# Batch 0 of a state-attention and Mish kernel: slot 0 in halves, low words rounded by GpSimd, steps in another order

## The chip, the cores and the metric

The kernel runs on one core of a Trainium2 chip. Its metric is device time in microseconds (us) of one execution. Engines are named as in the profile: PE is TensorE, PEld its weight loads, DVE VectorE, ACT ScalarE, POOL GpSimd, SP SyncE, which here issues the transfers.

## The reference, cut to what matters

```python
def _attn_ref(x, state):                     # x [8, 8, 512, 64], state [8, 8, 32, 64]
    scores = scale * x @ state^T             # softmax over the 32 states: a
    xread = a @ state                        # 512 rows of each batch
    scores2 = scale * state @ x^T            # softmax over the 512 tokens: a2
    sread = a2 @ x                           # 32 rows of each batch
    return concatenate([xread, sread], axis=2)

def _moe_ref(x, w_in, w_out):                # x [4352, 512]: the above, heads side by side
    h = x @ w_in                             # w_in [512, 2048], given as 64-bit floats
    g = h * tanh(softplus(h))                # Mish
    return g @ w_out                         # w_out [2048, 512], given as 64-bit floats
```

Eight batches of 512 + 32 rows go through the attention and then through the two products.

## The kernel before, in words

**Products.** The hidden width of 2048 is cut into 8 slots of 256 columns. For a batch and a slot the first product is not `xread @ w_in`: the kernel multiplies the state with the slot's columns of `w_in` (a slice, `sw`, tiles `swp`, `swh`, `swl`) and then with the softmax weights (tiles `ah`, `al`). Every fp32 operand of the big products is split into a high and a low part of type fp32r, and a product is three matmuls: high x high, high x low, low x high. The first product of a slot (`gemm1`, tiles `ph`) is two halves of 128 hidden columns with 6 matmuls of 512 columns each, in two PSUM banks (`ps_h`, two buffers). Mish (`take_g`, ScalarE) turns each half into its half of `g`; VectorE splits `g` into `gh` and `gl` (`high_g`, `low_g`). The second product (`gemm2`, tiles `acc`) adds the slot to four accumulators, one for each 128 tokens: 4 x 6 matmuls with the slot's `w_out`, itself split (`wo`).

**Weights.** `w_in` and `w_out` come as 64-bit floats, seen as pairs of 32-bit words. Once, during batch 0, every slot's share of each (1 MB, 128 x 1024 pairs) is turned into fp32 in three steps: ScalarE scales the high word (`scale_high`), an engine rounds the low word (`round_low`, an instruction over every second word), and VectorE joins the two (`join_words`, which reads both). `w_out` is then split by VectorE (`high_w_out`, `low_w_out`); `w_in` goes into the slices. SP issues the loads in one order: x of batch 0, `wir` 0, `wor` 0, `wir` 1, `wir` 2, `wor` 1, `wir` 3, `wor` 2, `wir` 4, `wor` 3, `wir` 5, x of batch 1, `wor` 4, 6, 5, `wir` 6, 7, `wor` 7. `wir` 4 to 7 reuse the buffers of `wir` 0, 1, 4, 5 and wait until these have been joined; `wor` 6 and 5 lie where `wir` 2 and 3 were.

**Batch 0 is an order written out by hand.** `InOrder` chains the instructions of PE, DVE and ACT in the order in which the Python code issues them. The code walks a list of step names; a step that is a generator goes on to its next `yield` each time its name comes. In a name, letters stand for the work and the number for the slot:

- `x`, `st`, `sc`, `tr`, `ex`, `no`, `pr`: attention of batch 0 (transposing x and the state, scores, exponentials, norms, weights `ah` and `al`); in capitals that of batch 1; `mm`, `ee`, `et`, `sr`, `rt`: its other softmax and `sread`
- `hi`, `ho`: high words of `w_in` or `w_out` (ScalarE); `ci`, `co`: low words by ScalarE; `di`, `do`: by VectorE; `ji`, `jo`: joining (`jo` comes twice, the second time for the high part); `lo`: low part of `w_out`
- `sw`: a slice (PE, then ScalarE's `swh`, then VectorE's `swl`); `p`: first product; `m`: Mish, then `gh`; `lg`: `gl`; `g`: one token tile of the second product; `next`: the first slice of batch 1
- `fillN`: N matmuls into an accumulator that is written anew later

In the order before, all low words but `di2`, `do1` and `do2` are rounded by ScalarE, and `fill6` stands between `p0` and `p1`.

**From batch 1 on** a loop over batches (`key`) and slots (`j`) issues the work. Besides the products, a slot may have a *visit*: slices (`sw_slice`), scores (`sc`), transposes (`et`) or `sread` matmuls (`sr`) of this or the next batch, which PE runs between the two halves of a slot's second product. In batch 1 the visits are those of slots 1 (slice 2), 2 (`et`), 3 (slice 4 and `sr`), 4 (`sc`), 5 (slice 6), 6 and 7.

The numbers in front of the lines are those of the profile. Nearly all instructions are recorded at L66, where `InOrder` issues them, so groups are told apart by their tiles.

Of the kernel before, what the change touches and what calls it, by code (L numbers as in the profile page):

```python
# [73 lines left out]
def state_attention_mish_kernel(ctx, tc, x, state, w_in, w_out, out):  # L74

    nc = tc.nc
    pe, dve, act = (InOrder(tc, e) for e in (nc.tensor, nc.vector, nc.scalar))
    nc.scalar.preload_act_table_set("exp_and_others")
# [71 lines left out]

    def round_low(raw, by_vector=False):
        lw = raw[..., 0]
        if by_vector:
            dve.tensor_scalar(lw, lw, 0.876 * 2.0 ** -29, 0.49, ALU.mult, ALU.add)
        else:
            last["words"] = act.activation(lw, lw, AF.Copy, scale=0.876 * 2.0 ** -29, bias=0.49)

    def join_words(raw, to):
        lw, hw = raw[..., 0], raw[..., 1]
        last["join"] = dve.scalar_tensor_tensor(  # L160
            to.bitcast(U32), hw, 3, lw, ALU.logical_shift_left, ALU.bitwise_or)
# [25 lines left out]

    def join_w_out(j, raw):
        w = pool.tile([P, 2, DM], F32, tag="wt", name=f"w_{j}", bufs=1)
        join_words(raw, w)  # L190
        return w

    def high_w_out(j, w):
        wo[j] = const.tile([P, 2, 2, DM], F32R, tag=f"wo{j}", name=f"wo_{j}")
        last["woh"] = dve.tensor_copy(wo[j][:, :, 1], w)
# [310 lines left out]
    def split_g(key, g):  # L506
        gh, gl = high_g(key, g)
        low_g(g, gh, gl)
        return gh, gl

    def high_g(key, g):
        gh = pool.tile([P, W], F32R, tag="gh", name=f"gh_{key}")
        gl = pool.tile([P, W], F32R, tag="gl", name=f"gl_{key}")
        dve.tensor_copy(gh, g)
        return gh, gl

    def low_g(g, gh, gl):
        dve.tensor_sub(gl, g, as_f32(gh))
# [3 lines left out]

    def gemm1(b, j, aT, sw):
        swh, swl = sw[j]
        phs = []
        for k in range(2):
            ph = ps_h.tile([P, 512], F32, tag="ph", name=f"ph_{b}_{j}_{k}")
            seq = []
            for kc in range(2):
                hi, lo = aT[kc]  # L530
                h, l = (t[:, kc, k * P:(k + 1) * P] for t in (swh, swl))
                seq += [(h, hi), (h, lo), (l, hi)]

# [111 lines left out]
    def by_tiles(j):  # L645
# [64 lines left out]
    for key, j in slots:  # L710
# [104 lines left out]
```

## Time and profile before

| | |
|---|---|
| median of 3 runs | 660.05 us (659.44 to 663.44) |
| profiled execution, device time | 659.24 us |
| its span, first to last instruction | 657.4 us |
| PE / PEld busy | 649.0 / 519.6 us |
| DVE / ACT / POOL busy | 337.8 / 259.1 / 0.7 us |
| bytes moved by DMA | 42.05 MB, 64 GB/s in the mean |

A row of the groups reads: line, engine, operation, output tile <- input tiles, shapes, count | busy us, mean ns of one | idle time of the engine ahead of it, and what ended it. A row of the timeline reads: start, duration, engine, line, operation, tiles, count, and in brackets the idle time ahead. The chain of work lists start, duration and what the end of the run was waiting for at that time. Matmuls overlap in the records: one of 128x512 is shown with some 390 ns, while 12 of them in a row take 2.72 us.

### The profile page before, as it was taken

The page shows a single profiled execution, that of the slowest core. Times are in us where ns is not written, and L with a number is a line of the kernel's source. Part 1 is how long each engine was busy: PE and PEld are TensorE (multiplying, and loading weights), DVE is VectorE, ACT ScalarE, POOL GpSimd, SP SyncE. Part 2 cuts the span into 40 slices and gives each one's busy share as a digit, 9 for nine tenths or more (in the row PEclk, how much of TensorE's full clock was granted, in tenths as well). Part 3 has the DMA queues.
Part 4 walks back from the last instruction along what each step waited for, and adds up shares of the span by engine and source line. Part 5 has one row for each costly group of instructions (what it writes and reads, how often), then busy time and mean ns, then how long its engine had stood idle before and what let it go on. Part 6 is the DMA issues. An engine that isn't in the chain of part 4 may idle for free.

```text
span 657.4 us, 10826 instructions
## 1 busy us (share of the span) xinstructions
PE 649.0 (99%) x4550; PEld 519.6 (79%) x4550; DVE 337.8 (51%) x517; ACT 259.1 (39%) x412; POOL 0.7 (0%) x6
## 2 busy tenths in 40 slices
PE   8999999999999999999999999999999999999997
PEld 5777777777778877787778887787778899878885
DVE  4979994356447344644437245544537345232222
ACT  4988853245315313442325222532235334131110
POOL 0000000000000000000000000000000000000000
PEclk9999999999999999999999999999999999999999
DMA  9975303400034002410033003400110001000001
GB/s 330 409 249 188 49 14 89 107 7 1 33 71 99 1 1 79 83 41 1 33 80 90 1 1 91 106 7 1 54 50 27 1 1 64 1 17 18 1 0 64
DMA packets 80672, 42.05 MB, mean 64 GB/s; under 512 B 61808, under 2 KB 70256, under 8 KB 80624
## 3 DMA queue, kind: packets, MB, share of 16 engines
q1 hardware_dynamic: 80192, 41.18, 21.5%
q8 instruction: 35, 0.57, 0.4%
q10 hardware_dynamic: 432, 0.20, 0.1%
q14 instruction: 13, 0.11, 0.0%
HBM read 32.44 MB, written 8.91 MB: 63 GB/s over the span
## 4 chain that ended last, share of the span: by engine, by line
PE 96%; DMA 1%; ACT 1%; SPq 1%; DVE 1%; issue 0%; ACTq 0%
PE acc L66 54%; PE ph L66 26%; PE swp L66 5%; PE ph_s L66 4%; PE acc_s L66 3%; DMA wir<-in_moe_w_in_dram 1%; PE srp L66 1%; PE sc L66 1%; PE e2p L66 1%; SPq L124 0%; ACT wir L66 0%; SPq L173 0%; DVE w_in_sb L66 0%; DVE gl L66 0%; ACT xT L66 0%
## 5 line engine op out<-in xcount | busy, mean ns | idle before, releaser
L66 PE MATMUL acc<-wo,gh 128*128 128x512 f32 x1024 | 320.0, 394 | 0.0
L66 PEld LDWEIGHTS acc<-wo,gh 128*128 128x128 f32 x1024 | 189.2, 188 | 47.0 <-issue 8.6
L66 PE MATMUL acc<-wo,gl 128*128 128x512 f32 x512 | 199.5, 390 | 0.0
L66 ACT ACTIVATE g<-ph 128x512 f32<-128x512 f32 x128 | 72.4, 596 | 198.1 <-DVE gl L66 172.9
L66 PEld LDWEIGHTS acc<-wo,gl 128*128 128x128 f32 x512 | 96.1, 188 | 20.6
L66 DVE CAST gh<-g 128x1024 fp32r<-128x1024 f32 x64 | 43.7, 683 | 113.9 <-PE acc L66 109.9
L66 DVE TENSOR_TENSOR gl<-g,gh 128x1024 fp32r<-128x1024 f32 x64 | 78.3, 1223 | 4.9 <-DVE sm L66 0.4
L66 PE MATMUL ph<-ah,swh 128*128 128x512 f32 x256 | 79.1, 391 | 0.0
L66 PE MATMUL ph<-ah,swl 128*128 128x512 f32 x256 | 78.6, 389 | 0.0
L66 PE MATMUL ph<-al,swh 128*128 128x512 f32 x256 | 78.5, 389 | 0.0
L66 DVE TENSOR_TENSOR swl<-swp,swh 128x512 fp32r<-128x512 f32 (+1 forms) x72 | 41.1, 624 | 68.1 <-ACT swh L66 68.1
L66 PEld LDWEIGHTS ph<-ah,swl 128*128 128x128 f32 x256 | 48.0, 188 | 10.0
L66 PEld LDWEIGHTS ph<-al,swh 128*128 128x128 f32 x256 | 48.1, 188 | 10.0
L66 PEld LDWEIGHTS ph<-ah,swh 128*128 128x128 f32 x256 | 47.6, 188 | 10.5 <-ACT ah L66 0.4
L66 ACT ACT_TABLE_LOAD x35 | 44.9, 1283 | 16.5 <-DVE gl L66 14.9
L66 ACT CAST swh<-swp 128x512 fp32r<-128x512 f32 (+1 forms) x72 | 34.2, 548 | 38.4 <-PE swp L66 38.4
L66 PE MATMUL swp<-w_in_sb,bd 64*32 64x256 f32 x1024 | 34.5, 381 | 0.4 <-ACT xT L66 0.2
L66 PEld LDWEIGHTS swp<-w_in_sb,bd 64*32 64x32 f32 x1024 | 17.4, 106 | 13.6 <-issue 7.7
L66 DVE TENSOR_REDUCE nm<-scs 128x1 f32<-128x512 f32 x16 | 10.3, 678 | 34.7 <-ACT scs L66 34.7
L66 ACT COPY o<-acc 128x512 f32<-128x512 f32 (+1 forms) x17 | 9.4, 562 | 41.8 <-PE acc L66 37.4
L66 DVE STREAM_TRANSPOSE xT<-xq 128x512 f32<-128x512 f32 x24 | 24.1, 1067 | 3.1 <-PE e2p L66 3.1
L66 DVE COPY o<-acc 128x512 f32<-128x512 f32 x16 | 11.0, 685 | 21.0 <-PE acc L66 15.8
(84 smaller groups left out, 473.6 us busy)
## 6 DMA issues: line engine op xcount, KB each, us to landing
x<-in_x_dram SPq DMA_DIRECT2D x32, 256.0 KB, 4.1
wir<-in_moe_w_in_dram SPq DMA_DIRECT2D x16, 512.0 KB, 10.0
wor<-in_moe_w_out_dram SPq DMA_DIRECT2D x16, 512.0 KB, 6.7
out_dram<-o SPq DMA_DIRECT2D x31, 256.0 KB, 2.4
xq<-in_x_dram SPq DMA_DIRECT2D x192, 32.0 KB, 2.3
sn<-in_state_dram SPq DMA_DIRECT2D x28, 32.0 KB, 2.1
out_dram<-o_s SPq DMA_DIRECT2D x8, 64.0 KB, 1.7
out_dram<-o SPq DMA_DIRECT2D x1, 128.0 KB, 2.7
```

The source lines that it names most:

```text
L66: made = method(*args, **kwargs)
```

## The change

- Slot 0 is worked in halves: joining, the first product, Mish, the split and the second product have steps of their own for each half (`jia`, `jib`, `joa`, `job`, `pa`, `pb`, `ma`, `mb`, `la`, `lb`, `ga`, `gb`, `wha`, `whb`, `loa`, `lob`). The words of `w_in` of slots 0 and 1 and of `w_out` of slot 0 are scaled and rounded in halves too. `ga0` uses the first 128 hidden columns and `gb0` the others.
- `gi`, `go` (with `a`, `b` for halves) are low words rounded by GpSimd, which has its own chain (`pool_e`). In the new order GpSimd does, one after the other, gia0 gib0 gia1 gib1 gi2 gi3 go1 go2 go5 gi5 go6 go4 gi6 gi7; ScalarE keeps `w_out` 0 (halves), `w_in` 4 and `w_out` 7, VectorE `w_out` 3.
- The list of steps has a new order. `fill6` now stands behind the slice of slot 0, ahead of the softmax weights; four fills stand ahead of the transposes of the scores.
- In batch 1 slice 6 moves from slot 5 to slot 3, beside slice 4, and `sr` from slot 3 to slot 4, beside `sc`.

```diff
     nc = tc.nc
-    pe, dve, act = (InOrder(tc, e) for e in (nc.tensor, nc.vector, nc.scalar))
+    pe, dve, act, pool_e = (InOrder(tc, e) for e in (nc.tensor, nc.vector, nc.scalar, nc.gpsimd))
...
-    def round_low(raw, by_vector=False):
+    def round_low(raw, by_vector=False, by_pool=False):
         lw = raw[..., 0]
-        if by_vector:
+        if by_pool:
+            pool_e.tensor_scalar(lw, lw, 0.876 * 2.0 ** -29, 0.49, ALU.mult, ALU.add)
+        elif by_vector:
...
-    def join_w_in(e, raw):
-        join_words(raw, w_in_sb[:, :, e * 2 * P:(e + 1) * 2 * P])
+    def join_w_in(e, raw, c=slice(0, NC)):
+        join_words(raw[:, c], w_in_sb[:, c, e * 2 * P:(e + 1) * 2 * P])
...
-    def join_w_out(j, raw):
-        w = pool.tile([P, 2, DM], F32, tag="wt", name=f"w_{j}", bufs=1)
-        join_words(raw, w)
+    def join_w_out(j, raw, c=slice(0, 2), w=None):
+        w = pool.tile([P, 2, DM], F32, tag="wt", name=f"w_{j}", bufs=1) if w is None else w
+        join_words(raw[:, c], w[:, c])
...
-    def gemm1(b, j, aT, sw):
+    def gemm1(b, j, aT, sw, ks=(0, 1)):
         swh, swl = sw[j]
         phs = []
-        for k in range(2):
+        for k in ks:
             ph = ps_h.tile([P, 512], F32, tag="ph", name=f"ph_{b}_{j}_{k}")
...
+    def join_o_half(o, c):
+        wfull[o] = join_w_out(o, rawo[o], slice(c, c + 1), wfull.get(o))
+
+    def first_half(j, k):
+        if k == 0:
+            phs[j] = [None, None]
+        phs[j][k] = gemm1(0, j, aTs[0], sw, (k,))[0]
+
+    def mish_half(j, k):
+        if k == 0:
+            gs[j] = (new_g(f"0_{j}"), *new_parts(f"0_{j}"))
+        g, gh, gl = gs[j]
+        take_g(g, k, phs[j][k])
+        yield
+        dve.tensor_copy(gh[:, k * 512:(k + 1) * 512], g[:, k * 512:(k + 1) * 512])
+
+    def low_half(j, k):
+        low_g(*(a[:, k * 512:(k + 1) * 512] for a in gs[j]))
+
+    def by_tiles_half(j, k):
+        for t in range(NT):
+            gemm2(0, [2 * j + k], *(a[:, k * 512:(k + 1) * 512] for a in gs[j][1:]), NT, (t,))
+            yield
+
+    def high_w_half(o, k):
+        if o not in wo:
+            new_wo(o)
+        dve.tensor_copy(wo[o][:, k, 1], wfull[o][:, k])
+
+    def low_w_half(o, k):
+        dve.tensor_sub(wo[o][:, k, 0], wfull[o][:, k], as_f32(wo[o][:, k, 1]))
+
+    a2, b2, a1, b1 = slice(0, 2), slice(2, 4), slice(0, 1), slice(1, 2)
+
...
+        "gi": lambda i: round_low(raws[i], by_pool=True), "go": lambda o: round_low(rawo[o], by_pool=True),
+        "gia": lambda i: round_low(raws[i][:, a2], by_pool=True), "gib": lambda i: round_low(raws[i][:, b2], by_pool=True),
+        "goa": lambda o: round_low(rawo[o][:, a1], by_pool=True), "gob": lambda o: round_low(rawo[o][:, b1], by_pool=True),
+        "pa": lambda j: first_half(j, 0), "pb": lambda j: first_half(j, 1),
+        "ma": lambda j: mish_half(j, 0), "mb": lambda j: mish_half(j, 1),
+        "la": lambda j: low_half(j, 0), "lb": lambda j: low_half(j, 1),
+        "ga": lambda j: by_tiles_half(j, 0), "gb": lambda j: by_tiles_half(j, 1),
+        "wha": lambda o: high_w_half(o, 0), "whb": lambda o: high_w_half(o, 1),
+        "loa": lambda o: low_w_half(o, 0), "lob": lambda o: low_w_half(o, 1),
...
-            x0 x0 x1 x1 st st x2 x2 x3 x3 sc acc sc sc sc sc ci0 tr0 tr1 hi0 tr0 tr0 ex0 tr1 tr1 fill2
-            ex1 ci1 ji0 sw0 no sw0 sw0 fill2 no hi1 pr0 ho0 pr0 ji1 pr1 pr1 co0 fill2 pr0 pr1 sw1 jo0
-            sw1 p0
-            m0 ho1 fill6 jo0 sw1 hi2 m0 lo0 lg0 p1
-            do1 di2 ji2 jo1 g0 g0 sw2 mm0 m1 hi4 sw2 hi3 jo1 g0 sw2 ci3 lo1 m1 lg1 g0 p2
-            g1 ji3 g1 ho2 mm1 do2 jo2 ee0 ee1 sw3 ee0 g1 g1 sw3 et0 m2 ee1 ci4 co3 sw3 et0 p3
-            m2 jo2 et1 lg2 lo2 m3 et1 sr0 ho3 g2 ji4 sw4 ho5 sr0 g2 g2 g2 sr1 jo3 sw4 m3 sw4 jo3 ci5 ho4
-            hi5 hi6 co5 lo3 sr1 p4
-            co4 ji5 sw5 sw5 lg3 ST g3 m4 sw5 g3 jo4 X1 jo4 p5
-            lo4 rt X1 X2 ci6 g3 rt m4 ji6 lg4 X0 rt X2 m5 X0 X3 sw6 X3 jo5 jo5 sw6 co6 lo5 g3 SC g4 sw6
-            m5 SC lg5 SC TR0 ho6 TR0 g4 p6
-            EX0 TR1 TR1 g4 jo6 g4 ci7 hi7 EX1 ji7 g5 g5 ho7 m6 sw7 jo6 sw7 NO NO g5 sw7 m6 PR0 g5 next
-            p7
-            lo6 lg6 co7 g6 next g6 m7 next jo7 PR1 PR1 jo7 PR0 g6 m7 PR1 PR0 lo7 lg7 g6
+            st x1 acc x0 x0 gia0 x2 x1 gib0 st x3 x2 x3 sc sc fill2 fill2 sc tr0 sc hib0 hia0
+            sc tr1 gia1 tr0 gib1 hob0 tr0 tr1 gi2 jib0 tr1 jia0 ex0 ex1 hib1 no sw0 hia1 cob0 fill6 sw0 no
+            pr0 jib1 pr1 gi3 pr0 sw0 pr1 hoa0 coa0 jia1 fill2 pr0 sw1 pr1 joa0 job0 pa0 pb0 ma0 sw1 ma0 la0
+            mb0 wha0 sw1 whb0 loa0 p1 lob0 mb0 hi2 lb0 ga0 ga0 ji2 ho1 ga0 m1 go1 jo1 ga0 sw2 mm0 sw2
+            jo1 sw2 hi4 ee0 m1 ho2 hi3 lo1 lg1 gb0 mm1 gb0 p2 gb0 ji3 gb0 ee0 do3 g1 g1 sw3 go2
+            ci4 ee1 jo2 g1 sw3 m2 g1 et0 sw3 p3 et0 jo2 ee1 m3 m2 go5 lg2 lo2 ho3 et1 et1 sr0
+            g2 sr0 m3 hi5 ji4 g2 jo3 sw4 sw4 g2 sr1 hi6 ho4 jo3 sw4 g2 lo3 gi5 ji5 ST p4 sw5
+            ho5 lg3 g3 sr1 sw5 go6 go4 X2 sw5 g3 X1 m4 X1 jo4 jo4 p5 rt g3 gi6 X0 gi7 m4
+            ji6 lg4 rt X3 lo4 sw6 rt X2 jo5 g3 X0 X3 SC jo5 m5 lo5 sw6 sw6 m5 SC SC hi7
+            lg5 ho6 TR1 g4 g4 g4 TR0 TR0 jo6 g4 co7 ho7 p6 ji7 TR1 EX0 g5 EX1 m6 sw7 sw7 NO
+            g5 NO g5 PR0 sw7 m6 PR1 PR0 g5 next next p7 jo6 PR0 lg6 lo6 jo7 PR1 jo7 g6 m7 g6
+            PR1 m7 g6 lg7 g6 next lo7
...
-        if key == 1 and j < 6 and j % 2:
-            beside += [sw_slice(key, j + 1)]
-        if key > 1 and j == 1:
+        if key == 1 and j == 1:
+            beside += [sw_slice(key, 2)]
+        if j == (3 if key == 1 else 1):
             beside += [sw_slice(key, 6, bank=first_bank), sw_slice(key, 4)]
         if more and j == 7:
...
-        if j == 3 and key < B - 1:
+        if j == (4 if key == 1 else 3) and key < B - 1:
             beside += [prev["sr"](k) for k in range(2)]
```

More of the change, by code (lines that the diff above doesn't have):

```diff
@@ L186, in load_w_out, with new_wo @@
         return raw
-    def join_w_out(j, raw):
-        w = pool.tile([P, 2, DM], F32, tag="wt", name=f"w_{j}", bufs=1)
-        join_words(raw, w)
-        return w
+    def join_w_out(j, raw, c=slice(0, 2), w=None):
+        w = pool.tile([P, 2, DM], F32, tag="wt", name=f"w_{j}", bufs=1) if w is None else w
+        join_words(raw[:, c], w[:, c])
+        return w
+    def new_wo(j):
+        wo[j] = const.tile([P, 2, 2, DM], F32R, tag=f"wo{j}", name=f"wo_{j}")
     def high_w_out(j, w):
-        wo[j] = const.tile([P, 2, 2, DM], F32R, tag=f"wo{j}", name=f"wo_{j}")
+        new_wo(j)
         last["woh"] = dve.tensor_copy(wo[j][:, :, 1], w)
@@ L509, in split_g, with new_parts @@
         return gh, gl
+    def new_parts(key):
+        return [pool.tile([P, W], F32R, tag=t, name=f"{t}_{key}") for t in ("gh", "gl")]
     def high_g(key, g):
-        gh = pool.tile([P, W], F32R, tag="gh", name=f"gh_{key}")
-        gl = pool.tile([P, W], F32R, tag="gl", name=f"gl_{key}")
+        gh, gl = new_parts(key)
         dve.tensor_copy(gh, g)
@@ L534, in gemm1 @@
             phs.append((ph, seq[::3] + seq[1::3] + seq[2::3]))
-        steps = [(k, i) for k in range(2) for i in range(6)]
+        steps = [(k, i) for k in range(len(ks)) for i in range(6)]
         if b == 0 and j < 2:
@@ L659, in state_attention_mish_kernel @@
         "do": lambda o: round_low(rawo[o], True), "jo": join_o,
+        "hia": lambda i: scale_high(raws[i][:, a2]), "hib": lambda i: scale_high(raws[i][:, b2]),
+        "cia": lambda i: round_low(raws[i][:, a2]), "cib": lambda i: round_low(raws[i][:, b2]),
+        "dia": lambda i: round_low(raws[i][:, a2], True), "dib": lambda i: round_low(raws[i][:, b2], True),
+        "jia": lambda i: join_w_in(i, raws[i], a2), "jib": lambda i: join_w_in(i, raws[i], b2),
+        "hoa": lambda o: scale_high(rawo[o][:, a1]), "hob": lambda o: scale_high(rawo[o][:, b1]),
+        "coa": lambda o: round_low(rawo[o][:, a1]), "cob": lambda o: round_low(rawo[o][:, b1]),
+        "doa": lambda o: round_low(rawo[o][:, a1], True), "dob": lambda o: round_low(rawo[o][:, b1], True),
+        "joa": lambda o: join_o_half(o, 0), "job": lambda o: join_o_half(o, 1), "wh": lambda o: high_w_out(o, wfull[o]),
+        "gi": lambda i: round_low(raws[i], by_pool=True), "go": lambda o: round_low(rawo[o], by_pool=True),
[7 more added lines that the diff above has]
+        "loa": lambda o: low_w_half(o, 0), "lob": lambda o: low_w_half(o, 1),
         "lo": lambda o: low_w_out(o, wfull.pop(o)),
```

## The prediction

> **What bounds the kernel now.** I read the page first, then the busy time by stretches of the first 100 us, then the chain of work through the same stretch, then the waits of TensorE, and last the order of instructions around each step that the change moves.
>
> ```profile
> span 657.4 us, 10826 instructions
> PE 649.0 (99%) x4550; PEld 519.6 (79%) x4550; DVE 337.8 (51%) x517; ACT 259.1 (39%) x412; POOL 0.7 (0%) x6
> ```
>
> TensorE works through 99% of the span, so the change can only win what TensorE loses, and the shares of the other engines over the whole run say nothing. The stretches do (columns: stretch, length, busy us and count of PE, PEld, DVE, ACT, POOL, granted clock, DMA share, GB/s):
>
> ```profile
> 5.00:15.00 10.00, 8.91 (x84) 5.09 (x82) 6.45 (x11) 5.16 (x9) 0.00 (x0) 1.00 1.04 394
> 15.00:35.00 20.00, 18.54 (x125) 14.48 (x119) 18.34 (x29) 19.88 (x26) 0.00 (x0) 1.00 1.05 399
> 35.00:45.00 10.00, 10.00 (x60) 7.57 (x60) 8.26 (x15) 7.48 (x13) 0.00 (x0) 1.00 0.85 316
> 45.00:65.00 20.00, 20.00 (x179) 15.09 (x178) 16.82 (x23) 17.94 (x25) 0.00 (x0) 1.00 0.51 167
> 65.00:100.00 35.00, 34.76 (x233) 26.24 (x232) 32.92 (x51) 23.90 (x36) 0.00 (x0) 1.00 0.21 35
> ```
>
> Batch 0 is the one stage where other engines are near their limit: ScalarE is busy 19.88 of 20 us from 15 to 35, VectorE 76.34 of 85 us from 15 to 100. GpSimd does nothing. Yet after 20 us TensorE hardly waits:
>
> ```profile
> 5.39 9.19 DMA wir<-in_moe_w_in_dram
> 19.69 2.92 PE ph L66 x12
> 22.61 1.34 PE acc L66 x12
> 23.95 2.74 PE ph L66 x12
> 26.69 2.72 PE acc L66 x12
> 65.99 1.15 PE swp L66 x16
> ...
> PE at L66 <- DVE e L66: 1.3, 2, 1.0
> PE swp L66 <- ACT xT L66: 0.2, 1, 0.2
> ```
>
> The first rows are the chain of work: `p0` ends at 22.61, 1.34 us of `fill6` follow, `p1` starts at 23.95 and the second product of slot 0 at 26.69. The last two are TensorE's waits up to 90 us: none long but those for the softmax before `p0`, and 0.2 us at 65.99. So the whole stake is when slot 0 gets through, and whether VectorE keeps up behind it.
>
> **Slot 0.** Up to `p0`:
>
> ```profile
> 16.10 0.76 DVE L66 TENSOR_TENSOR swl<-swp,swh 128x256 fp32r<-128x256 f32 x2
> 17.05 0.69 DVE L66 TENSOR_TENSOR e<-e,r 128x512 f32<-128x512 f32 x1
> 17.66 1.22 DVE L66 SCALAR_TENSOR_TENSOR w_in_sb<-wir 128x1024 uint32<-128x1024 uint32 x1
> 18.90 1.29 DVE L66 TENSOR_TENSOR al<-at,ah 128x512 fp32r<-128x512 f32 x2
> 20.96 1.28 ACT L66 ACT_TABLE_LOAD   x1
> 22.25 1.08 ACT L66 ACTIVATE g<-ph 128x512 f32<-128x512 f32 x2
> 23.98 1.22 DVE L66 TENSOR_TENSOR wo<-w,wo 128x1024 fp32r<-128x1024 f32 x1
> 25.12 1.22 DVE L66 TENSOR_TENSOR gl<-g,gh 128x1024 fp32r<-128x1024 f32 x1
> ```
>
> VectorE sets `p0`: last norm (17.05), joining `w_in` 1, `al` until 20.19. In the new order both norms stand ahead of `swl` (0.7 us), so the last one ends near 17.0 instead of 17.7 (0.7 earlier, less some 0.1 for four fills ahead of the score transposes and joins in halves); then `jib1`, `swl`, `jia1`, `al`, `al` cost 0.6 + 0.7 + 0.6 + 1.3 and end at 20.2, as now. So `p0` itself gains nothing: I take both halves from 19.6 to 22.3. `fill6` now stands ahead of it, where TensorE waits for the norms anyway (the 1.3 us above), so it costs nothing there; should the norms come earlier, it would cost up to its 1.34.
>
> Behind `p0` the gain begins. Half 0 ends near 21.0, its Mish near 21.7 and VectorE splits it at once; half 1's Mish ends at 23.1 (22.3 plus 0.2 and one instruction of 0.6). `p1` needs that bank: two matmuls at 22.3, the other ten from 23.1 at 0.23 each (2.72 over 12), end 25.4. VectorE from the end of `al`: two half joins (1.3), the split of half 0 (0.4 + 0.6), two half casts (0.4 each) around `swl` (0.7), two half `lo` (0.6 each): `loa0` ends at 24.7, 0.7 ahead of `ga0`. `ga0` then starts at 25.4 against 26.69: **a lead of 1.3 us**. It can be 0 if those 0.7 us and 1.3 more are lost on VectorE.
>
> **Roundings on GpSimd.**
>
> ```profile
> L66 ACT ACTIVATE wir<-wir 128x1024 f32<-128x1024 f32 (+1 forms) x15 | 16.8, 1152 | 0.2 <-DMA wir<-in_moe_w_in_dram 0.2
> L66 DVE TENSOR_SCALAR wor<-wor 128x1024 uint32<-128x1024 uint32 x2 | 1.4, 686 | 0.0
> L66 DVE TENSOR_TENSOR e<-e,r 128x512 f32<-128x512 f32 x16 | 10.9, 684 | 0.1
> 0.24 0.10 POOL L801 MEMSET const-float32-0.0<- 128x1 f32 x1 [0.24 <-issue]
> 0.73 0.20 POOL masks.py:197 MEMSET ident<- 128x128 f32 x1 [0.29 <-POOLq L801]
> 1.01 0.29 POOL masks.py:199 TENSOR_SCALAR_AFFINE_SELECT ident<-ident 128x128 f32<-128x128 f32 x1
> wir<-in_moe_w_in_dram SPq DMA_DIRECT2D x16, 512.0 KB, 10.0
> ```
>
> ScalarE gives up ten of thirteen whole roundings, 10 x 1.15 = 11.5 us, and VectorE two of three, 2 x 0.69 = 1.4. Neither is a term: TensorE does not wait for ScalarE from 20 to 65 us. Halves cost VectorE 2 x 0.68 against 1.22 where it works in one cycle per element, some 0.15 each, about 0.6 in all. What a rounding costs GpSimd no row shows. From 128x1 to 128x128 its instructions grow by 0.1 (MEMSET) to 0.19 us (AFFINE_SELECT), which over 1024 elements gives 0.9 to 1.6 us; I take 1.3, between two rows that fit equally badly. It hides as long as it lands ahead of its join. A slot's two transfers of 512 KB take 2.6 us at the 399 GB/s above; `wir` 1 ends at 14.58 (5.39 + 9.19), so by the order of the queue (`wir` 2, `wor` 1, `wir` 3) those land near 17.2, 19.8 and 22.4. `gib1` has until 17.0, a half may take 2.4; `gi3` and `go1` start at 22.4 ahead of `jo1` at 27.4, so one may take 2.5. By either end that is covered.
>
> The Trainium skill, "GPSIMD Engine Reference", section 7, has about 1.9 cycles per element at steps of 8 bytes, at 1.2 GHz; by it a rounding would take some 1.6 us, an estimate from that page, and the sum stays the same. No run here shows it.
>
> **The way from slot 1 to batch 1.** The order of products is as before (`p2` in the middle of slot 0's second product, then `g1`, `p3`, ...), so a lead stays as long as splits and slices come that much earlier. Two tight places:
>
> ```profile
> 58.84 1.09 ACT L66 ACTIVATE g<-ph 128x512 f32<-128x512 f32 x2
> 59.94 0.70 PE L66 MATMUL ph<-ah,swh 128*128 128x512 f32 x2
> 96.59 2.72 PE acc L66 x12
> 94.92 1.22 DVE L66 TENSOR_TENSOR gl<-g,gh 128x1024 fp32r<-128x1024 f32 x1
> L173 SPq DMA_DIRECT2D wir<-in_moe_w_in_dram x4: 367/424/469, 46.9 to 55.4; - x4
> DMA to landing us min/median/max: 3.7/4.2/4.7
> ```
>
> `p5` starts as Mish 4 ends. In the new order `hi6`, `ho4`, `ho5` and the slice copies of `sw5` stand ahead of `m4` on ScalarE, and `hi6` waits for `wir` 6, whose transfer waits for `ji4` to free its buffer: now at 46.9, landing within 4.7 us (last two rows: the four halves of `wir` 6 and 7). ScalarE then goes on at 51.6; three instructions of 1.05, a slice of 0.6, the table load of 1.3 and Mish of 1.1 end at 57.8, 0.8 ahead of the new `p5` at 58.6. If `ji4` comes later by more, `p5` moves with it. On GpSimd `go5` waits for `wor` 5, the last of the queue that keeps the DMA engines 0.85 busy from 35 to 45, and `gi5`, `go6`, `go4` wait behind it; four of 1.3 from 43.5 end at 48.7, and `ji5`, which needs the second of them, is done only near 55 now (it lets the second pair of halves go). And `gl` of slot 7 ends 0.45 us ahead of its product at 96.59, with VectorE 94% busy there. If VectorE gains nothing, that takes back up to 0.9 of 1.3. I keep 1.0.
>
> **Batch 1.**
>
> ```profile
> 140.33 1.02 PE swp L66 x32
> 141.36 2.94 PE acc L66 x12
> 177.61 1.89 PE swp L66 x64
> 179.49 2.99 PE acc L66 x12
> ```
>
> A visit of one slice costs 1.02 and lengthens the next product by 0.22 (2.94, against the 2.72 of the row at 26.69); two together cost 1.89 + 0.27, as batch 2 has it. Twice 1.24 less 2.16 is **0.3 us**. `srp` moves to the visit of `sc`, a visit that is there anyway. The bank that the second slice borrows must be free before the next `ph`; batch 2 does this at 177.61 with nothing lost; if not, 0.3 is gone.
>
> **Sum.** The profiled execution took 659.24 us (span 657.4). Less 1.0, less 0.3, less the 0.2 wait at 65.99: 657.7. The median of the runs shown, 660.05, lies 0.8 above that execution; on its scale, 658.5.
>
> **Rivals.**
> *VectorE and GpSimd shut each other out (slower).* If an instruction of one holds up the other for its full length, every rounding costs VectorE time. Nothing in this trace speaks for or against it, GpSimd being idle; but VectorE's 76 of 85 us leave little room. `gi2` from 17.6 holds `jia1` by 0.6; `gi3`, `go1`, `go2` fall among the eleven instructions that lead to `loa0`: 3 x 1.3. `loa0` then ends at 24.7 + 4.5 = 29.2 and `ga0` starts some 0.3 earlier: 2.2 later than now. `go5`, `gi5`, `go6`, `go4` come together near 43 to 50, ahead of `ji4`, and two of them add up to 2.6. 659.2 + 2.2 - 0.5 + (0 to 2.6) = 660.9 to 663.5, 0.8 more on the runs' scale; by the ends of the rounding, 0.9 and 1.6 us, the whole case spans 660 to 667 there. It decides from 0.7 us lost on VectorE ahead of `loa0`, and turns to a loss from 2. The Trainium skill, "SBUF — State Buffer", section "Who interferes with whom", says that a VectorE instruction with two SBUF inputs, or in a two-port mode, and a GpSimd instruction that reads SBUF fully block each other; by that rule this rival comes true. No run here shows it.
>
> *VectorE takes the lead back.* Slot 7's place above, or halves dearer than reckoned: 659.0 to 660.5 on the runs' scale.
>
> *It doesn't do what it says:* a rounding beyond 2.5 us, or a slow first one, leaves `gia0` (due at 12.5, data near 7) or `go1` late, ScalarE being free in vain: 660 to 664.
>
> **How the numbers follow.** Forecast (656.8 to 659.4) 0.45; shutting out (660 to 667) 0.35; lead taken back 0.13; slow roundings 0.07. The range reaches from 656.5 to 665.5. One per cent, about what a measurement tells here, is 6.6 us: faster by more needs 653.4, which only a `p0` some 4 us earlier would give, 0.02; slower by more needs 666.7, the far end of the first rival, 0.10; within 0.88.
>
> **What would show it.** `p0` ending at 22.3 and `ga0` starting at 25.4; GpSimd instructions of 0.9 to 1.6 us; joins of 1.22 us as before, against joins and `gl` stretched while GpSimd runs (first rival); `hi6` starting by 51.6; one visit of 64 `swp` in batch 1. The prediction is wrong if VectorE's mean times grow or TensorE waits after 25 us.

## The result, and the profile after

| | before | changed |
|---|---|---|
| median of 15 runs each, side by side | 659.86 us (659.09 to 663.44) | 663.33 us (661.93 to 663.74) |
| ratio | | 1.0044, 95% interval 1.0034 to 1.0055 |
| profiled execution / its span | 659.24 / 657.4 us | 663.64 / 661.9 us |

The change makes the kernel slower by some 3 us, where the forecast was 658.5. The time lies in the middle of the first rival, "VectorE and GpSimd shut each other out" (660 to 667).

The page of the changed kernel:

```profile
span 661.9 us, 10857 instructions
PE 650.8 (98%) x4550; PEld 520.1 (79%) x4550; DVE 342.5 (52%) x522; ACT 249.3 (38%) x406; POOL 18.2 (3%) x20
```

VectorE was to lose two roundings (1.4 us) and to pay some 0.6 us for halves; it shows 4.7 us more, 342.5 against 337.8. TensorE is busy 1.8 us longer in a span that grew by 4.5, so most of the loss is waiting. The stretches show where (columns as in the prediction):

```profile
15.00:35.00 20.00, 17.64 (x120) 12.16 (x119) 19.20 (x34) 15.75 (x25) 6.08 (x6) 1.00 1.05 401
45.00:65.00 20.00, 18.10 (x169) 13.35 (x168) 16.84 (x20) 12.20 (x18) 8.94 (x6) 1.00 0.46 157
65.00:100.00 35.00, 34.83 (x232) 25.96 (x231) 34.09 (x52) 21.95 (x35) 1.07 (x1) 1.00 0.23 38
```

From 15 to 35 us ScalarE got 4 us freer (15.75 against 19.88), while VectorE went from 18.34 to 19.20. From 45 to 65 TensorE lost 1.9 us where it had lost nothing. Its waits up to 110 us (what waited for whom, us in total, times, longest), and the places in its timeline:

```profile
PE swp L66 <- DVE w_in_sb L66: 2.2, 2, 1.1
PE srp L66 <- DVE swl L66: 0.8, 1, 0.8
PE ph L66 <- DVE swl L66: 0.6, 1, 0.6
PE swp L66 <- ACT e L66: 0.5, 1, 0.5
```

```profile
20.68 0.67 PE L66 MATMUL swp<-w_in_sb,bd 64*32 64x256 f32 x16 [1.13 <-DVE w_in_sb L66]
27.17 1.30 PE L66 MATMUL ph<-ah,swl 128*128 128x512 f32 x4 [0.55 <-DVE swl L66]
52.42 0.67 PE L66 MATMUL swp<-w_in_sb,bd 64*32 64x256 f32 x16 [1.06 <-DVE w_in_sb L66]
55.52 0.65 PE L66 MATMUL srp<-x,e2T 128*32 128x64 f32 x32 [0.84 <-DVE swl L66]
```

But for one of 0.2 us for Mish, every wait after the softmax is for VectorE: for joined words (`w_in_sb`) and for a slice's low part (`swl`). Now VectorE and GpSimd at the same places:

```profile
19.57 0.96 DVE L66 SCALAR_TENSOR_TENSOR w_in_sb<-wir 128x512 uint32<-128x512 uint32 x1
24.06 1.49 DVE L66 TENSOR_TENSOR gl<-g,gh 128x512 fp32r<-128x512 f32 x1
25.48 1.31 DVE L66 CAST wo<-w 128x512 fp32r<-128x512 f32 x1
26.71 0.74 DVE L66 TENSOR_TENSOR swl<-swp,swh 128x256 fp32r<-128x256 f32 x2
48.67 1.57 DVE L66 CAST gh<-g 128x1024 fp32r<-128x1024 f32 x1
50.16 2.12 DVE L66 SCALAR_TENSOR_TENSOR w_in_sb<-wir 128x1024 uint32<-128x1024 uint32 x1
52.20 2.20 DVE L66 SCALAR_TENSOR_TENSOR w<-wor 128x1024 uint32<-128x1024 uint32 x1
56.84 1.22 DVE L66 SCALAR_TENSOR_TENSOR w_in_sb<-wir 128x1024 uint32<-128x1024 uint32 x1
58.34 1.18 DVE L66 TENSOR_TENSOR gl<-g,gh 128x1024 fp32r<-128x1024 f32 x1
```

```profile
18.82 1.17 POOL L66 TENSOR_SCALAR wir<-wir 128x1024 uint32<-128x1024 uint32 x1 [1.94 <-DMA wir<-in_moe_w_in_dram]
23.89 1.12 POOL L66 TENSOR_SCALAR wir<-wir 128x1024 uint32<-128x1024 uint32 x1 [3.91 <-DMA wir<-in_moe_w_in_dram]
25.09 2.68 POOL L66 TENSOR_SCALAR wor<-wor 128x1024 uint32<-128x1024 uint32 x2
46.81 1.68 POOL L66 TENSOR_SCALAR wor<-wor 128x1024 uint32<-128x1024 uint32 x1 [19.05 <-DMA wor<-in_moe_w_out_dram]
48.57 1.12 POOL L66 TENSOR_SCALAR wir<-wir 128x1024 uint32<-128x1024 uint32 x1
49.77 3.57 POOL L66 TENSOR_SCALAR wor<-wor 128x1024 uint32<-128x1024 uint32 x2
58.34 2.15 POOL L66 TENSOR_SCALAR wir<-wir 128x1024 uint32<-128x1024 uint32 x1 [5.00 <-DMA wir<-in_moe_w_in_dram]
```

Lay the two side by side. From 46.81 to 53.34 GpSimd works without a break, and in that time a cast takes 1.57 us and two joins take 2.12 and 2.20. At 56.84, with GpSimd quiet, a join takes 1.22 as before. The three together are 2.8 us longer (0.69 for such a cast in the page's groups). GpSimd is held up as well: a rounding alone takes 1.12, but two took 3.57. It is the same at 23.89 to 27.77: a half `gl` takes 1.49 and a half cast 1.31 (0.69 and 0.42 in no_gi2 below, where GpSimd is idle there). `swl`, which reads PSUM, keeps its 0.75 in the middle of that (26.71).

The rows also show who waits for whom. A VectorE instruction that begins while a rounding runs is longer by what is left of the rounding, less some 0.14 us: the join at 19.57 finds 0.42 us left (18.82 + 1.17 is 19.99) and takes 0.28 more than the 0.68 of such a half, `gl` at 24.06 finds 0.95 and takes 0.80 more, the cast at 48.67 finds 1.02 and takes 0.88 more. So it is in the profiles of all kernels for the 46 joins, casts, norms and splits that began with over 0.1 us of such a GpSimd instruction left: 0.13 to 0.17 us less than what was left. Left out are instructions that read PSUM and the two that begin together at 58.34. There `gl` keeps its time (1.18) and the rounding takes 2.15; likewise the 30 joins, casts, norms and splits that began before a rounding kept theirs within 0.05. Whichever begins first runs at its own length, and the other waits.

Two rows of ScalarE's timeline show what else changed:

```profile
13.56 0.67 ACT L66 ACTIVATE wor<-wor 128x512 f32<-128x512 f32 x1 [1.24 <-DMA wor<-in_moe_w_out_dram]
58.27 1.16 ACT L66 ACTIVATE wir<-wir 128x1024 f32<-128x1024 f32 x1 [4.46 <-DMA wir<-in_moe_w_in_dram]
```

`hob0` waits 1.24 us for the load of `wor` 0 and holds up the exponentials of the softmax behind it (`ex0` at 14.12 instead of 12.93, 0.47 of it from the scores being later). That depends on when the load lands: in early_back and no_pool below, with the step in the same place, `hob0` starts at 12.27 and 12.29 and `ex0` comes 1.91 us behind the first maximum, as before the change (2.63 here). `hi6` starts at 58.3, where I had reckoned with 51.6.

### The profile page after: what moved, and what is told of

It reads as the page before. It is cut to its first block, busy times and chain, and to the rows that moved or that the text cites. A ratio compares the mean times of both kernels' runs of the same rounds, so it can differ in the third digit from the quotient of the medians.

```text
span 661.9 us, 10857 instructions
## 1 busy us (share of the span) xinstructions
PE 650.8 (98%) x4550; PEld 520.1 (79%) x4550; DVE 342.5 (52%) x522; ACT 249.3 (38%) x406; POOL 18.2 (3%) x20
## 4 chain that ended last, share of the span: by engine, by line
PE 92%; DVE 2%; DMA 2%; ACT 1%; issue 1%; SPq 1%; ACTq 0%; DVEq 0%
PE acc L66 52%; PE ph L66 25%; PE swp L66 5%; PE ph_s L66 3%; PE acc_s L66 3%; DMA wor<-in_moe_w_out_dram 1%; PE srp L66 1%; PE sc L66 1%; PE e2p L66 1%; DVE w_in_sb L66 1%; DMA wir<-in_moe_w_in_dram 1%; ACT wor L66 0%; DVE wo L66 0%; DVE gh L66 0%; DVE s L66 0%
## 5 line engine op out<-in xcount | busy, mean ns | idle before, releaser
L66 DVE CAST gh<-g 128x1024 fp32r<-128x1024 f32 (+1 forms) x65 | 44.7, 688 | 112.0 <-PE acc L66 108.3
L66 DVE TENSOR_TENSOR gl<-g,gh 128x1024 fp32r<-128x1024 f32 (+1 forms) x65 | 79.3, 1220 | 4.8
```

The costliest lines, as they stand in the source:

```text
L66: made = method(*args, **kwargs)
```

## Where the time goes, stage by stage

The start of TensorE's first product of a slot is called p, of its second product g. `mx` is VectorE's first maximum of the softmax: counting from it leaves out when the first transfers land, which differs from one execution to the next (10.8 to 12.8 us), but not when later ones do, such as `wor` 0. All numbers are us from the timelines of one profiled execution of each kernel; the kernels are explained in the next section.

| kernel | mx to p0 | p0 to g1 | g1 to g2 | g2 to p5 | p5 to p8 | ratio to before |
|---|---|---|---|---|---|---|
| before | 8.60 | 15.90 | 10.59 | 13.83 | 33.70 | |
| changed | 9.79 | 16.47 | 10.58 | 16.34 | 33.79 | 1.0044 |
| pool_only | 9.91 | 16.81 | 10.63 | 15.08 | 34.41 | 1.0043 |
| hob_late | 9.13 | 16.63 | 10.60 | 16.61 | 33.75 | 1.0053 |
| early_back | 8.99 | 15.19 | 11.34 | 16.43 | 33.76 | 1.0030 |
| late_back | 9.80 | 16.63 | 10.60 | 14.49 | 33.76 | 1.0016 |
| all_back | 9.70 | 15.19 | 11.34 | 14.34 | 33.35 | 1.0012 |
| no_gi2 | 8.70 | 15.35 | 11.17 | 14.33 | 33.38 | 0.9996 |
| mixed | 8.71 | 15.37 | 11.25 | 14.91 | 34.46 | 1.0026 |
| no_pool | 8.95 | 16.02 | 10.58 | 18.68 | 35.28 | 1.0066 |
| visit_fill | 8.85 | 15.65 | 10.91 | 13.85 | 33.78 | 0.9986 |

In the new order 0.45 us of transposes (`X2`) stand ahead of p5 instead of behind it, so 14.28 there is as good as 13.83 before.

## The experiments

**The hold-up by itself.** The kernel before, with 24 GpSimd instructions on a tile that nothing else touches; in the second kernel they only write.

```diff
+    def beside_dve(_):
+        s = scratch[..., 0]
...
+        pool_e.tensor_scalar(s, s, 0.876 * 2.0 ** -29, 0.49, ALU.mult, ALU.add)   # dummy_read
+        pool_e.memset(s, 0)                                                      # dummy_write
```

> The kernel before, and 24 GpSimd roundings of 128x448 words in a scratch tile that nobody else touches, two behind each of 12 VectorE steps of slots 0 to 4 (z0 to z11). No other engine waits for them. Theory (VectorE and GpSimd hold each other up for whole instructions): each of some 0.6 us stretches the VectorE instruction that meets it, joins from 1.22 to 1.8 or more, casts from 0.69 to 1.3; VectorE busy grows by 6 to 14 us up to 60 us, TensorE begins to wait, and the time is 662 to 668 against 659.9. Rival (they do not hold each other up, and the long joins of the changed kernel are waits for the rounded words): every VectorE instruction keeps its time, and the kernel stays within 0.7 us of the one before.

> As dummy_read, with MEMSET of 128x448 words instead of the rounding: GpSimd writes and reads nothing. Theory in the form that only shared reading matters for two-input instructions: joins, gl and lo (two inputs from SBUF) keep their 1.22 us, casts of 0.69 (two elements a cycle) are still stretched; VectorE busy grows by 1 to 5 us and the time is 660 to 663. If any GpSimd instruction holds up any VectorE instruction, it is as slow as dummy_read; if there is no hold-up at all, 659.9.

The instructions did not stand where I wanted them, beside twelve chosen steps of VectorE: they ran one after another, up to 20.7 and 15.5 us. So the reads are tested on the softmax up to the start of slot 0 and the writes on the first half of the softmax, and neither meets a cast. Times: reading 661.15 us, ratio 1.0020 (1.0009 to 1.0031); writing 660.35, 1.0013 (1.0004 to 1.0023); the intervals overlap, so the times don't tell the two apart. The timelines do. GpSimd and VectorE with reads:

```profile
2.13 18.55 POOL L66 TENSOR_SCALAR scratch<-scratch 128x448 uint32<-128x448 uint32 x24
...
12.63 1.33 DVE L66 SCALAR_TENSOR_TENSOR w_in_sb<-wir 128x1024 uint32<-128x1024 uint32 x1
13.89 0.67 DVE L66 TENSOR_REDUCE s<-e 128x16 f32<-128x512 f32 x1
15.91 1.09 DVE L66 TENSOR_TENSOR e<-e,r 128x512 f32<-128x512 f32 x1
16.92 0.74 DVE L66 TENSOR_TENSOR swl<-swp,swh 128x256 fp32r<-128x256 f32 x2
18.60 1.60 DVE L66 SCALAR_TENSOR_TENSOR w_in_sb<-wir 128x1024 uint32<-128x1024 uint32 x1
```

and with writes alone:

```profile
1.98 13.49 POOL L66 MEMSET scratch<- 128x448 uint32 x24
...
12.32 1.23 DVE L66 SCALAR_TENSOR_TENSOR w_in_sb<-wir 128x1024 uint32<-128x1024 uint32 x1
15.34 0.69 DVE L66 TENSOR_TENSOR e<-e,r 128x512 f32<-128x512 f32 x1
```

Beside a GpSimd that reads, joins and norms, which take two inputs from SBUF, grow by 0.1 to 0.4 us; the reductions and `swl` do not. Beside one that only writes, the one join that it meets keeps its time; the norm meets only the last 0.13 us of the writes and says little. Writes are not free for everything: a small instruction with one input (`s<-s`, 128x16) took 0.28 us at 15.22 beside one, 0.13 before. mx to p0 is 9.64 with reads and 8.46 with writes. No data and no buffer is shared, so the hold-up is one of the two engines. Why the writing kernel is slower than before by its ratio, some 0.9 us, stays open: its profiled span is that of before (657.4). Both kernels begin with a memset of the tile, which puts the identity matrix at 1.75 instead of 1.01 us; that was not tried apart.

**GpSimd without the new order.** The kernel before, with the same twelve roundings on GpSimd, its steps otherwise where they were.

```diff
-    ... sc acc sc sc sc sc ci0 tr0 ... ex1 ci1 ji0 ... do1 di2 ji2 ... ci3 ... do2 ... ci5 ... co5 ... co4 ... ci6 ... co6 ... ci7
+    ... sc acc gi0 gi1 gi2 gi3 go1 go2 go5 gi5 go6 go4 gi6 gi7 sc sc sc sc tr0 ...
```

> The kernel before, whole slots, old order and old batch 1; only the same twelve roundings are done by GpSimd, ahead of everything else on its queue. Theory (hold-up): VectorE's joins, casts and lo near 18 to 28 and 45 to 55 are stretched by up to 1.1 us each, and although ScalarE is freed of ten roundings the time does not fall: 660 to 663. Rival (freeing ScalarE pays, the loss comes from the halves and the new order): 657 to 659.

662.95 us, ratio 1.0043 (1.0024 to 1.0062): as slow as the whole change. The profiled execution, 663.99, is 4.8 us longer than that of before. Half a microsecond or so of it is an input that landed late; the rest lies in the stages, 1.3 us from mx to p0, 0.9 from p0 to g1, 1.25 from g2 to p5 and 0.7 from p5 to p8:

```profile
24.39 2.99 POOL L66 TENSOR_SCALAR wor<-wor 128x1024 uint32<-128x1024 uint32 x2
...
26.35 2.11 DVE L66 TENSOR_TENSOR wo<-w,wo 128x1024 fp32r<-128x1024 f32 x1
```

The second row is the low part of slot 0's `w_out`, 1.22 us before. In the first 112 us VectorE waits for no result of GpSimd. The roundings alone cost what the change costs; neither the halves nor the order is needed for it.

**All roundings back at once.** The changed kernel with the twelve on ScalarE and VectorE, right behind the scaling of the same words or, by VectorE, ahead of the join.

```diff
-    gia0 gib0 gia1 gib1 gi2 gi3 go1 go2 go5 gi5 go6 go4 gi6 gi7
+    cia0 cib0 cia1 cib1 di2 ci3 do1 do2 ci5 co4 co5 ci6 co6 ci7
```

> The changed kernel with its order and halves, GpSimd's twelve roundings given back: w_in 2, w_out 1 and 2 to VectorE right ahead of their join, the others to ScalarE right behind the high words. Theory (the hold-up costs 3 to 4 us, the order itself is good): joins and gl of 1.22 again, halves of 0.68, no wait of TensorE on swl near 27 nor on w_in_sb near 52, time 658.5 to 660.5. Rival (the halves and the new order are the loss): TensorE waits in the same places and the time stays at 662 to 664.

663.78 us, 1.0066 (1.0049 to 1.0083): slower still. This order is made for a free ScalarE. Its timeline and TensorE's:

```profile
55.34 2.16 ACT L66 ACTIVATE wir<-wir 128x1024 f32<-128x1024 f32 x2 [3.47 <-DMA wir<-in_moe_w_in_dram]
57.39 4.09 ACT L66 ACTIVATE wor<-wor 128x1024 f32<-128x1024 f32 x4
...
62.26 0.66 PE L66 MATMUL xTp<-ident,x 128*128 128x128 f32 x4 [3.00 <-DVE swl L66]
```

ScalarE waits 3.47 us for `wir` 6, then works off six instructions ahead of slice 5's copies, and TensorE waits 3.0 us for that slice; from 64 to 67 us its granted clock was then 0.50, which adds to the 18.68. (The profiled execution, 665.75, is the slowest of the four.) The experiment changes two things at once and does not tell the theories apart; the next ones give the roundings back in groups, at places where ScalarE is idle.

**The early three and the late four.** Both start from the changed kernel.

```diff
 early_back: ... hi3 [-gi3 +ci3] ... ho1 [-go1 +co1] ... [-go2 +do2] jo2 ...
 late_back:  ... sw4 [-gi5 +ci5] g2 sr1 [-go4 +co4] hi6 ... X1 m4 X1 [-go5 +co5] ... sw6 [-go6 +co6] ...
```

> The changed kernel, with three roundings taken from GpSimd between 23.9 and 27.8 us: w_in 3 and w_out 1 to ScalarE (behind hi3 and ho1), w_out 2 to VectorE (ahead of its join, 0.6 us there). GpSimd keeps the other nine. Theory (hold-up): gl of half 0 and the half casts behind it take 0.69 and 0.43 again instead of 1.49 and 1.31, TensorE's wait for swl near 27 goes, and slot 0's second product starts near 27.0 instead of 28.3; later hold-ups stay, so 661.9 to 663.0. Rival (the halves are the loss there): it starts at 28.3 as before and the time is 663 or more.

> The changed kernel, with the four roundings between 46.8 and 53.4 us given back to ScalarE (w_in 5, w_out 4, 5, 6) at places where it stood idle. Theory (hold-up): gh, ji4 and jo3 take 0.69, 1.22 and 1.22 instead of 1.57, 2.12 and 2.20, TensorE no longer waits 1.1 us for slice 4 at 52 and 0.8 us for swl at 55, and the second product of slot 2 to the first of slot 4 take 2 us less: 660.8 to 662.2. Rival (the order there is the loss: ScalarE stands still for wir 6): the waits move to p5, and the time stays within 0.7 us of 663.3.

early_back: 661.89 us, 1.0030 (1.0018 to 1.0042). late_back: 661.21 us, 1.0016 (1.0004 to 1.0028). The three early roundings cost 1.3 us from p0 to g1 (16.47 against 15.19) and save 0.8 from g1 to g2, so 0.5 in all. The profile of early_back is a further 0.8 shorter from mx to p0, where the edit changes nothing: its exponentials did not have to wait behind `hob0`. How much of the 1.4 us between the medians is due to the three roundings is therefore open. The four late ones cost 1.9 from g2 to p5. The same three VectorE instructions as above, in late_back:

```profile
48.42 0.68 DVE L66 CAST gh<-g 128x1024 fp32r<-128x1024 f32 x1
49.02 1.22 DVE L66 SCALAR_TENSOR_TENSOR w_in_sb<-wir 128x1024 uint32<-128x1024 uint32 x1
50.29 1.23 DVE L66 SCALAR_TENSOR_TENSOR w<-wor 128x1024 uint32<-128x1024 uint32 x1
```

They are at their old length, and TensorE's two waits there (1.06 and 0.84) are gone.

**`hob0` behind the exponentials.** One step of the changed kernel moved.

```diff
-    gib1 hob0 tr0 tr1 gi2 jib0 tr1 jia0 ex0 ex1 hib1
+    gib1 tr0 tr1 gi2 jib0 tr1 jia0 ex0 ex1 hob0 hib1
```

> The changed kernel, with one ScalarE step moved: hob0, which waits for w_out 0 to land at 13.5, behind the two exponentials instead of ahead of them. Theory (that wait delays the softmax): the first exponential starts near 13.1 instead of 14.2, the norms and p0 come some 0.8 to 1.1 earlier, and the time falls by 0.3 to 1.1, to 662.2 to 663.0. Rival (p0 is set by VectorE and GpSimd alone): p0 stays at 21.3 and the time at 663.3.

663.27 us, 1.0053 (1.0038 to 1.0068; 4 runs): no gain in time. In the profile `ex0` comes 1.91 us behind mx and mx to p0 is 0.66 us shorter (9.13), but the way from p0 to p5 is 0.45 longer, so that 0.2 is left at p8: the lead runs into the same roundings.

**Both ideas with few roundings.** GpSimd keeps the four halves of `w_in` 0 and 1 alone, `hob0` is late, `hi6` and `m4` change places.

```diff
-    gi2 gi3 go1 go2 go5 gi5 go6 go4 gi6 gi7
+    di2 ci3 co1 do2 co5 ci5 co6 co4 ci6 ci7
-    hi6 ho4 jo3 ... ho5 lg3 g3 sr1 sw5 ... X1 m4 X1
+    ho4 co4 jo3 ... sw5 ho5 hi6 lg3 g3 sr1 m4 sw5 co5 ... X1 X1
```

> The changed kernel without hold-up where VectorE is tight: GpSimd keeps the four halves of w_in 0 and 1, done by 17 us; hob0 behind the exponentials; the other roundings on ScalarE (w_in 3 to 7, w_out 0, 1, 4 to 7) and VectorE (w_in 2, w_out 2, 3), and ScalarE does hi6 and Mish 4 without standing still for wir 6. Theory (hold-up and ScalarE's two waits for transfers are the whole loss, the halves bring 1 us): slot 0's second product starts near 26 (26.7 before the change, 28.3 with it), and the time is 657.8 to 659.3, below both. Rival (halves and order cost by themselves): 660.5 to 663.

661.47 us, 1.0026 (1.0016 to 1.0037): in the rival's range, 2.2 us above the upper end of mine. The early part is as in no_gi2 below; from g2 to p5 it loses 0.6 against late_back's kind and from p5 to p8 1.1. It differs from no_gi2 in `ci4`, `hi6`, `m4` and in `w_in` 6 and 7 being on ScalarE; which of these costs the 1.7 us is not told apart. Its profile has two waits of TensorE there that no_gi2's has not, 0.40 us for slice 5 (60.81) and 0.68 for ScalarE's copies of x (68.65).

**Group by group to the end.** all_back joins early_back, late_back and hob_late; no_gi2 takes `w_in` 2 off GpSimd too, which then keeps the four halves, `gi6` and `gi7`.

```diff
 all_back: early_back + late_back + hob_late
 no_gi2:   all_back, and ... tr1 [-gi2] jib0 ... ga0 ga0 [+di2] ji2 ...
```

> The changed kernel with both groups of GpSimd roundings back on ScalarE and VectorE (early: gi3, go1, go2; late: go5, gi5, go6, go4) and hob0 behind ex1; the four halves of w_in 0 and 1, gi2 and gi6 stay on GpSimd. If the two costs that early_back (-1.4 us) and late_back (-2.1 us) showed are separate and add up, 663.3 - 3.5 = 659.8, with hob0's move anything from 0 to -0.7: 659.1 to 659.8, the time of the kernel before. p0 to g1 should take 15.2 us as in early_back and g2 to p5 14.5 as in late_back. Rival: ScalarE and VectorE, given back 7 roundings of 1.15 and 0.69 us, come late for some product in their turn, and the time stays at or above 661, as in the run named mixed.

> all_back with gi2 off GpSimd too: w_in 2 is rounded by VectorE right ahead of its join (di2), 0.69 us there. In the profile of all_back the half join at 18.82 took 1.61 us beside gi2 (18.43, 1.47 us), where half joins took 0.67 otherwise. If the hold-up sets p0 there, both half joins behind the norms now take 0.67, the way from the end of the last norm to the start of p0 is 0.9 us shorter (18.90 to 22.43, 3.5 us, becomes 2.6), and the time is 0.3 to 0.9 us below all_back's 660.7: 659.8 to 660.4, no measurable difference from the kernel before. Rival: di2 in VectorE's chain behind p1 costs what the hold-up did (0.69), or p0 is set by the landing of the first transfers alone; then the time stays at 660.4 to 661.0.

all_back: 660.66 us, 1.0012 (0.9998 to 1.0026), 0.9 us above the upper end of what I expected; its stages are those expected (15.19 and 14.34), and p0 is late. The sum had taken early_back's 1.4 us whole, though 0.8 of its profile's gain lies ahead of p0. no_gi2: 659.80 us, 0.9996 (0.9984 to 1.0009). GpSimd and VectorE ahead of p0, in all_back:

```profile
18.43 1.47 POOL L66 TENSOR_SCALAR wir<-wir 128x1024 uint32<-128x1024 uint32 x1 [1.91 <-DMA wir<-in_moe_w_in_dram]
...
18.82 1.61 DVE L66 SCALAR_TENSOR_TENSOR w_in_sb<-wir 128x512 uint32<-128x512 uint32 x1
```

and in no_gi2, with two rows of its later timeline:

```profile
17.72 0.68 DVE L66 SCALAR_TENSOR_TENSOR w_in_sb<-wir 128x512 uint32<-128x512 uint32 x1
...
37.80 1.23 DVE L66 SCALAR_TENSOR_TENSOR w_in_sb<-wir 128x1024 uint32<-128x1024 uint32 x1 [1.89 <-ACT wir L66]
...
39.17 0.67 PE L66 MATMUL swp<-w_in_sb,bd 64*32 64x256 f32 x16 [0.53 <-DVE sm L66]
```

One rounding that begins 0.4 us ahead of a half join makes it 0.93 us longer, and mx to p0 goes from 9.70 to 8.70 without it. With these eight roundings off GpSimd and `hob0` late the changed kernel has the time of the kernel before. Of the six left on it, one holds up a half join (1.12 us at 13.52), for which TensorE waits 0.34 us, and one a cast (1.52 at 60.07), for which it does not wait. The last two rows are why it is not faster: the lead of the halves (p0 to g1 15.35 against 15.90) is gone by g2, since the join of `w_in` 3 waits for ScalarE's words, and TensorE 0.53 us for that join (37.80 + 1.23 is 39.03; the wait is put down to `sm`, a small instruction that ends with it). From p0 to g2 it is 26.52 us, and 26.49 before.

**The visit alone, and a filler moved.** The kernel before with the change in batch 1; and the same with `fill6` left out and four fills put into TensorE's wait ahead of the second weights (17.8 us).

```diff
 visit_only: slice 2 at slot 1, slices 6 and 4 at slot 3, sr at slot 4 (as in the change)
 visit_fill: ... hi1 pr0 ho0 pr0 [+fill4] ji1 pr1 ... m0 ho1 [-fill6] jo0 ...
```

> The kernel before with the change in batch 1 alone: slice 2 of batch 1's sw at visit 1, slices 6 and 4 at visit 3, sr at visit 4. If my 0.3 us for the visit holds (p5 to p8 took as long before as after, and the lag of the changed kernel fell from 4.8 us at p8 to 4.5 at the end), the first product of batch 1 (p8) starts where it did before (93.6), the rest of the run is 0.3 us shorter and the time 0.2 to 0.4 below that of the kernel before: some 659.5, a ratio of 0.9995. The rival, that the visit does nothing and the 0.3 came from batch 0's late end having left work done ahead, gives the time of before within 0.1 us.

> The kernel before with the batch 1 change, and with fill6 (12 idle-time matmuls, 1.26 us of TensorE between p0 and p1) taken out and four pairs... of such fillers put instead into TensorE's wait ahead of the second pair of transposes of e (16.77 to 17.80). If TensorE itself is the bound between p0 and g0, p1 starts 1.2 us sooner, g0 is held to the end of gl 0 (26.34 in the trace of before) and starts 0.6 to 1.2 us sooner; with the visit's 0.3 the time is 658.3 to 659.0. Rival: the lead is lost again at the next product (g1 waits for mish 1 on ScalarE behind the three table loads, or fill4 is longer than the wait and p0 starts later by what it exceeds it), and the time is that of the visit alone, 659.5.

visit_only: 660.34 us, 0.9998 (0.9984 to 1.0011): in time it cannot be told from nothing. In the profile it can: from the start of batch 1's slice 2 (103.56) to the end of the span (658.7) it is 555.14 us, against 555.44 before (101.96 to 657.4); in the changed kernel 555.19. Its p0 came late (mx to p0 9.91) behind a wait of 1.41 us at the weights, after which the granted clock was 0.50 for some 3 us; from g1 on every stage is as before.

visit_fill: 659.35 us, 0.9986 (0.9977 to 0.9995), the one version faster than both kernels. How it does it is not what I expected. g0 starts 0.63 us earlier (25.89), but `gl` ends only at 26.4; at g1 0.21 is left (35.31) and at p5 nothing (60.07 against 59.94). But eleven of its twelve runs lie between 658.99 and 659.98, where the kernel before has a third of its 29 above 660.5 (the twelfth, at 3693 us, is a disturbance, as visit_only had one). The mean granted clock that is on record for every run goes with this: the nine above 660.5 have 0.996 or 0.997, the other twenty 0.999 or 1.00, and of the eleven of visit_fill none is below 0.998 (nor of the twelve of no_gi2). Against those twenty, with a median of 659.7, visit_fill is 0.4 us faster, about what the visit gives. The rest of its gain goes with the absence of executions with a lowered clock. The wait at the weights is 0.40 us instead of 1.03. That the lower clock comes from that wait would fit the profile of visit_only, which has 0.996 in the mean and lost its clock right behind it; no profile of the kernel before with a lower clock is at hand, so it stays a guess.

## Why the prediction was wrong

**The step that failed** is the one on roundings: "It hides as long as it lands ahead of its join." That treats GpSimd as a free engine and asks only when its result is there. Its results were in time, and its running was what cost: VectorE, the engine with 76 of 85 us busy, waited for roundings under way, 0.80 and 0.89 us ahead of `ga0` and 2.8 us on end from 48.67. The mechanism was written down as a rival, with its place and price, and got 0.35 against 0.45. I had no row for it, GpSimd being idle before, and gave the sum the case that needs no interaction. The Trainium skill, "SBUF — State Buffer", section "Who interferes with whom", said plainly which instructions would be held up: those with two SBUF inputs, by GpSimd instructions that read, and those in a two-port mode. The runs agree: joins 1.22 to 2.2, norms 0.69 to 1.09, casts 0.69 to 1.57 beside reads, reductions and PSUM-reading `swl` unchanged, one join unchanged beside writes. Which mode an instruction runs in, no trace here shows. A rule of the Trainium skill about the very pair of engines that a change sets to work together deserved more than 0.35.

**The rival's price** was near. I had 2.2 us later at `ga0` and up to 2.6 from the late four: g0 started at 28.3, 1.8 later than in the timeline of before (26.5), and the late four cost 1.9. The early part was made of other things than I thought, though: `gi2` 0.4 to 1.0 ahead of p0, `gi3`, `go1`, `go2` 1.3 less the 0.8 that they save at g2, and `hob0`. That the total came out in the middle of the rival's range is in part luck.

**A rounding** was to take 0.9 to 1.6 us, 1.3 taken: 1.12 alone, 0.65 for a half. The 1.6 that followed from the Trainium skill, "GPSIMD Engine Reference", section 7, is too high here. "It doesn't do what it says" did not come about: no join waited for GpSimd alone.

**p0** was to be as before, 19.6. It came at 21.28: 0.47 from the scores being later, 0.66 from `hob0` (hob_late), 0.43 from `gi2` (hob_late against no_gi2), the rest below 0.2. The first two are matters of when transfers landed in that execution. I had gone through GpSimd's and VectorE's queues and not through ScalarE's, where a step that waits for a transfer now stood ahead of the exponentials. The 0.7 by which the norms move up are there in no_gi2 (mx to the end of the last norm 6.1 us, 6.7 before), and the half joins use them up, as reckoned.

**The lead of 1.3 us at `ga0`** was 0.8 without roundings (p0 to g0 6.1 against 6.9) and 0.55 at g1. "A lead stays as long as splits and slices come that much earlier": they did not, and at g2 it was 0. That is the second rival, and without GpSimd it would have been the whole story. So the sum was wrong even with GpSimd set aside: of its terms the 0.3 of the visit held, and the 0.2 us wait at 65.99 is gone in the changed kernel but stands in no_gi2 (0.24 us at 66.88).

**`hi6`** came at 58.3, not 51.6: `ji4` ended at 52.3 rather than 46.9, itself held up 0.9 us and behind a cast held up as much, and `wir` 6 landed 6 us behind it, not 4.7. p5 still did not wait, since m4 ended at 64.4 and TensorE was itself late, at 64.7.

**The visit**: 0.3 forecast; 0.25 to 0.34 in the profiles of the five kernels that were read for it (changed, visit_only, visit_fill, all_back, no_gi2).

## What to carry to other kernels

Before work goes to an idle engine, ask which engine it will hold up, and how full that one is: here 12 roundings, some 14 us of GpSimd's time had they run alone, cost the kernel 3 us, because VectorE waited for part of them. Count for each instruction that meets one up to the whole rounding, and nothing where it begins first. Where the Trainium skill names such a pair, the hold-up belongs into the sum, and a term of zero needs a row that shows it. And a lead at one product is worth nothing until the next join, slice and split are seen to come earlier too; in a chain kept by hand the queue of the engine that got freer must be read for new waits as well.

## What was unexpected of the hardware

GpSimd pays too: two roundings took 3.57 us instead of 2.24 beside VectorE's joins, and one 2.15 at 58.34. The stretch of a VectorE instruction was nearly a whole rounding once (0.93 us, all_back) and only 0.10 us of a join once (dummy_read, at 12.63). What was left of the GpSimd instruction when the other began makes the difference: 1.08 us in all_back (18.43 + 1.47 less 18.82), and 0.26 in dummy_read, whose read there is

```profile
12.31 0.58 POOL L66 TENSOR_SCALAR scratch<-scratch 128x448 uint32<-128x448 uint32 x1
```

The granted clock of TensorE fell in two of the profiles, both times behind a wait. One stretch each, of visit_only and of no_pool (the clock is the third number from the end):

```profile
19.00:21.00 2.00, 2.00 (x21) 0.96 (x21) 1.73 (x4) 1.69 (x4) 0.00 (x0) 0.50 1.03 398
```

```profile
64.00:67.00 3.00, 3.00 (x10) 2.41 (x10) 2.94 (x4) 1.00 (x2) 0.00 (x0) 0.50 0.00 0
```

In stretches of 1 us visit_only, whose wait of 1.41 us ended at 18.03, shows 1.00 up to 18, then 0.63, 0.50, 0.50, 0.66, and 1.00 again from 22 on. In no_pool, whose wait of 3.0 us ended at 62.26, it is 1.00 up to 63, then 0.80, 0.50 from 64 to 67, and 0.99. So in both TensorE ran at half its clock for some 3.4 us and began to soon after the wait, not in it; by these figures that costs some 1.7 us, an estimate. It is not a matter of the wait's length alone: all_back waited 1.77 us, up to 21.84, and kept 1.00.
